# Pooled-key attention with a maxout layer: four of the first batch's twelve kv tiles are added by the loading DMAs

## The chip, the cores and the metric

The kernel runs on one core of a Trainium2 chip. The metric is the device time of one execution in microseconds (us); the median of 3 runs stands for a kernel. The engines are TensorE (PE in the profile; PEld is its weight load), VectorE (DVE), ScalarE (ACT), GpSimd (POOL) and SyncE (SP), which in this kernel only issues DMAs. The 16 DMA engines of the core are shared by everything that any engine issues.

## The reference

Keys and values are the same tensor: `kv` (4 batches, 384 x 32 positions, 128 channels), averaged over 4 x 4 windows and multiplied by `w_sr`. The queries attend to these 768 keys, and the result goes through a maxout layer with three weight matrices and an output matrix.

```
kv_pool = kv.reshape(B, H // 4, 4, W // 4, 4, C).mean(axis=(2, 4))
k = v = kv_pool.reshape(B, -1, C) @ w_sr
s = 1 / sqrt(C) * (q @ k.T);  a = exp(s - s.max(-1));  a /= a.sum(-1) + 1e-09
x = a @ v
out = max(x @ w1, x @ w2, x @ w3) @ w_out
```

There are 4 x 12288 queries, C is 128, and the hidden width is 768. All inputs and outputs are float32.

## The kernel before, in words

The queries are worked off in 96 groups of 512 (`G`). For each group there are score matmuls (token `S`), softmax on VectorE and ScalarE (`m`, `e`), splits into pairs of float16 (`c`, `l`), a DMA that transposes the weights of attention, the product with the values (`X`), the hidden layer (`H`, `R`, `M`, `C`, `L`) and the output product (`O`). Products are made of three float16 matmuls (high by high, high by low, low by high), which keeps nearly float32 accuracy.

The order of all work is written out by hand. Three tables of tokens, `START` (line 168), `STEADY` and `END`, are run by `run` (line 1165); each token calls one function. Every engine is wrapped in `InOrder` (line 98), so that it takes its instructions in the order in which the tokens issue them. All wrapped instructions carry line 106 of that helper, and are told apart in the profile by the names of their tiles. The chains between engines, the semaphores, follow from the tiles that an instruction reads and writes.

The change lies in `START`, in the preparation of the first batch's keys (class `Keys`, line 408). The batch's kv rows are cut in three parts s = 0, 1, 2 (`KS` = 3), and each part in four tiles i = 0 to 3, the four rows of a pooling window. A tile `pieces[s, i]` is 128 partitions of 1024 float32 (512 KB): two halves u of four neighbouring positions by 128 channels. What `START` does with them:

- `kv.s.i` (`load`, line 430): SP issues the load of a tile into a buffer of the pool `kvp` (13 buffers, line 82). Tile 2.2 is loaded in two halves. The same pool takes the eight 384 KB tiles of the layer's weights (`wd.n.h`, `load64`, line 248), which SP loads behind the kv tiles.
- `add.s.i.n` (`add`, line 442): tile n is added onto tile i, on VectorE, or on GpSimd with a `!`.
- `gat.s.i` (`gather`, line 464): TensorE multiplies each of a tile's eight 128 x 128 blocks with the identity and accumulates in PSUM. This sums what is left of the part and turns it, so that channels lie on partitions. One tile is 16 matmul instructions in the profile.
- `gd` and `gj`: ScalarE copies the sum out of PSUM (`pooled`), TensorE multiplies it by `w_sr`. `gp`, `gt`, `tops`, `sized` find a power of two for scaling, `gh` and `gl` split the keys into float16 pairs `k_hi`, `k_lo`. The first scores (`S`) need all parts.
- `fold`, `gb`: tile 2.0 is the late one (`LATE`, line 78); it is summed with 2.1 and 2.3 on VectorE, folded to half its width, and gathered last.
- `z` (`stir`, line 853): a matmul whose result nobody reads.

Before the change, parts 1 and 0 come first. SP loads 0.1, 1.3, 1.1, 1.0, 1.2, 0.3, 0.2, 0.0 and then the four tiles of part 2. In part 1 `add.1.2.3` adds tile 1.3 onto 1.2 (VectorE), `add.1.0.1!` adds 1.1 onto 1.0 (GpSimd), and 1.0 and 1.2 are gathered. In part 0 `add.0.2.3`, `add.0.0.1` and `add.0.0.2` sum all four tiles on VectorE into 0.0, which is gathered. GpSimd has before this the scaling of three half tiles of queries (`qc`), and after it the signs of the weights (`wn`). Later batches' keys are made in another way (`keys_step`, line 1141), spread over the steady part, and are not touched.

The weights are unpacked from pairs of 32-bit words by VectorE and ScalarE (`wm`, `ws`, `wl`, `wn`; tiles `w_e`), in `START`, between the softmax of the first groups.

Of the kernel before, what the change touches and what calls it, by code (L numbers as in the profile page):

```python
# [16 lines left out]
ALU = mybir.AluOpType  # L17
# [4 lines left out]
def kernel(  # L22
# [32 lines left out]
    B, N, C = q.shape  # L55
    _, HH, WW, _ = kv.shape
    R = 4
# [3 lines left out]
    P = 128  # L61
    NKT = NK // P
    NFT = DF // P
    G = 512
# [14 lines left out]
    KH, KW, KS, KU = 32, WB // 2, HB // 32, 2  # L79
# [6 lines left out]
    qp = ctx.enter_context(tc.tile_pool(name="qp", bufs=3))  # L86
# [11 lines left out]
    class InOrder:  # L98
# [9 lines left out]
    pe, dve, act, pool, sp_dma = (  # L108
        InOrder(e) for e in (nc.tensor, nc.vector, nc.scalar, nc.gpsimd, nc.sync)
    )  # L110
# [25 lines left out]
    def spread(out, t, n, start, stop):  # L136

        mm(out=out, lhsT=upper(t)[:, n:n + 1].to_broadcast([P, P]), rhs=upper(ident), start=start, stop=stop)
# [19 lines left out]
    wo = [const.tile([P, NFT // 2, 2, C], F16, name=f"wo{h}") for h in range(2)]  # L158
# [8 lines left out]
    TURNED = 2  # L167
    START = (
# [27 lines left out]
    )  # L196
    STEADY = (
# [28 lines left out]
    def sr_weights():  # L226
        e = prep.tile([C, C], F32, name="sr_e")
        dve.tensor_scalar(
            out=e.bitcast(I32), in0=wsr_sb.bitcast(I32), scalar1=0x7FFFFFFF, scalar2=None, op0=ALU.bitwise_and
        )  # L230
        ps = spare(True)
        mm(out=ps[:, :C], lhsT=ones, rhs=e, start=True, stop=True)
        pow2(col_row, ps[:, :C])
        dve.reciprocal(out=e, in_=col_row)
        dve.tensor_tensor(out=wsr_sb, in0=wsr_sb, in1=e, op=ALU.mult)
        ps = spare(True)
        mm(out=ps[:, :1], lhsT=col_row[:1], rhs=ones[:1, :1], start=True, stop=True)
        times(col, ps[:, :1], 1.0)
        times(col_ones, ones, col)
        W["sr"] = True  # L240
# [23 lines left out]
    tops = {}  # L264

    class Weights64:
# [13 lines left out]
        def load(self):  # L280
            self.r1, self.r0 = load64(self.w, self.h, self.wide)
# [126 lines left out]
    class Keys:  # L408
# [21 lines left out]
        def load(self, s, i, u=None):  # L430
            src = kv[self.b].rearrange("(s h i) (w r) c -> s i h w (r c)", s=KS, i=R, w=KW)[s, i]
            self.width.update({(s, i, n): R for n in (range(KU) if u is None else (u,))})
            if u is None:
                self.pieces[s, i] = kvp.tile([P, PIECE], F32, name="kv_piece")
                sp_dma.dma_start(out=self.pieces[s, i], in_=src)
                return
            if (s, i) not in self.pieces:
                self.pieces[s, i] = kvp.tile([P, PIECE], F32, name="kv_piece")
            part = slice(u * PIECE // KU, (u + 1) * PIECE // KU)
            sp_dma.dma_start(out=self.pieces[s, i][:, part], in_=src[:, :, part])  # L440

        def add(self, s, i, n, on=dve, us=slice(None)):
            view = lambda m: self.pieces[s, m].rearrange("p (u x) -> p u x", u=KU)[:, us]
            on.tensor_tensor(out=view(i), in0=view(i), in1=view(n), op=ALU.add)
            if self.first:
                assert all(self.width[s, i, u] == self.width[s, n, u] for u in range(KU)[us])
                assert not {(x, u) for x in (i, n) for u in range(KU)[us]} - self.left[s] - (self.late if s == LATE[0] else set())
                self.left[s] -= {(n, u) for u in range(KU)[us]}
# [404 lines left out]
    def stir(on=None):  # L853

        if on:
            return
        any_ = ones.bitcast(F16)
        mm(
            out=spare(False), lhsT=any_[:, :P], rhs=any_[:, :1].to_broadcast([P, G]), start=True, stop=True,
        )  # L860
# [235 lines left out]
    def start(token):  # L1096

        k, on = KT[0], dve if token[-1] == "!" else None  # L1100
        name, *n = token.rstrip("!").split(".")
        n = [int(x) for x in n]
        both = {"": slice(None), 0: slice(0, 1), 1: slice(1, 2)}
        if name == "sr":
            sr_weights()
        elif name == "kv":
            k.load(*n)
        elif name == "add":
            k.add(*n[:3], on=pool if on else dve, us=both[n[3] if n[3:] else ""])
        elif name == "fold":  # L1110
            k.fold(*n[:3], on=pool if on else dve, us=both[n[3] if n[3:] else ""])
        elif name == "gat":
            s, i, *u = n
            k.gather(s, i, u or range(KU))
        elif name in KEYS:
            getattr(k, KEYS[name])(*n, *([on] if on else []))
        elif name[0] == "w" and name[1:] in WEIGHTS:
            getattr(W[n[0], n[1]], WEIGHTS[name[1:]])(*([on] if on else []))
        elif name == "z":
            stir(on)  # L1120
        elif name in AIDS:
            AIDS[name](*n)
        else:
            step(name, on)
# [40 lines left out]
    def run(rows):  # L1165
        for row in rows:
            for token in row.split():
                start(token)
# [37 lines left out]
```

## Time and profile before

| | us |
|---|---|
| median of 3 runs | 1979.29 |
| lowest and highest run | 1977.48, 1981.5 |
| the profiled execution | 1975.92 |
| its span, first to last instruction | 1974.1 |

The profile is of that one execution. A row of the timeline or of the chain begins with its start in us from the span's start and its length in us; then engine, line, operation, written tile <- read tiles, shapes, and in brackets the idle time before it with what ended it. A row of the stretches gives for `A:B` the length, then the busy us (and the number of instructions) of PE, PEld, DVE, ACT and POOL, the granted TensorE clock, the mean busy share of the DMA engines and the GB/s that they moved. A row of a tile's instructions gives minimum, median and maximum length in ns, and first and last start; for DMA issues the line "DMA to landing" gives the us from the issue to the arrival of the last byte. A row of the groups gives busy us, mean ns of one, and the idle time before with what ended it. In the rows of DMA issues the last number is the median us to landing.

### The profile page before, as it was taken

The page shows a single profiled execution, that of the slowest core. Times are in us where ns is not written, and L with a number is a line of the kernel's source. Part 1 is how long each engine was busy: PE and PEld are TensorE (multiplying, and loading weights), DVE is VectorE, ACT ScalarE, POOL GpSimd, SP SyncE. Part 2 cuts the span into 40 slices and gives each one's busy share as a digit, 9 for nine tenths or more (in the row PEclk, how much of TensorE's full clock was granted, in tenths as well). Part 3 has the DMA queues.
Part 4 walks back from the last instruction along what each step waited for, and adds up shares of the span by engine and source line. Part 5 has one row for each costly group of instructions (what it writes and reads, how often), then busy time and mean ns, then how long its engine had stood idle before and what let it go on. Part 6 is the DMA issues. An engine that isn't in the chain of part 4 may idle for free.

```text
span 1974.1 us, 29441 instructions
## 1 busy us (share of the span) xinstructions
PE 1957.0 (99%) x9793; PEld 956.0 (48%) x9793; DVE 1447.5 (73%) x2523; ACT 1493.3 (76%) x2629; POOL 1311.5 (66%) x960
## 2 busy tenths in 40 slices
PE   7999999999999999999999999999999999999999
PEld 5444444444444444444444444444444444444444
DVE  8867777777767777777667777777766676766677
ACT  5777777777777777777777777777777777777775
POOL 4576766666667666766676677766676666666653
PEclk9999999999999999999999999999999999999999
DMA  9688777667677778766768767866776666766673
GB/s 280 126 157 165 154 148 142 142 132 143 128 149 166 155 145 160 144 129 136 137 132 166 155 147 157 169 122 128 137 143 137 131 127 127 146 122 125 131 129 81
DMA packets 842696, 283.97 MB, mean 144 GB/s; under 512 B 816048, under 2 KB 817200, under 8 KB 842544
## 3 DMA queue, kind: packets, MB, share of 16 engines
q1 hardware_dynamic: 842544, 282.09, 71.0%
q8 instruction: 77, 1.26, 0.3%
q14 instruction: 75, 0.61, 0.1%
HBM read 53.54 MB, written 25.17 MB: 40 GB/s over the span
## 4 chain that ended last, share of the span: by engine, by line
PE 98%; DMA 1%; DVE 0%; ACT 0%; SPq 0%; POOL 0%; issue 0%; ACTq 0%; POOLq 0%
PE ps_h L106 38%; PE ps_o L106 22%; PE ps_x L106 19%; PE ps_s L106 19%; DMA kv_piece<-in_kv_dram 0%; DMA aT<-ahl 0%; DMA kv_piece<-in_moe_w_dram 0%; SPq L106 0%; POOL kv_piece L106 0%; DVE w_e L106 0%; DVE ahl L106 0%; DVE mx L106 0%; ACT a L106 0%; ACT pooled L106 0%; ACT ahl L106 0%
## 5 line engine op out<-in xcount | busy, mean ns | idle before, releaser
L106 POOL TENSOR_TENSOR hl<-h,hh 128x512 f16<-128x512 f32 x474 | 565.9, 1199 | 508.0 <-ACT hh L106 496.8
L106 POOL TENSOR_TENSOR ahl<-a,ahl 128x768 f16<-128x768 f32 x378 | 627.7, 1681 | 99.5 <-ACT ahl L106 73.1
L106 DVE SCALAR_TENSOR_TENSOR h<-ps_h,h 128x512 f32<-128x512 f32 x575 | 396.4, 689 | 371.1 <-PE ps_h L106 213.2
L106 ACT ACTIVATE h<-ps_h 128x512 f32<-128x512 f32 x575 | 342.6, 596 | 282.9 <-PE ps_h L106 272.5
L106 PE MATMUL ps_h<-xh,d_hi 128*128 128x512 f16 x1150 | 435.8, 379 | 0.1
L106 PE MATMUL ps_h<-xl,d_hi 128*128 128x512 f16 x1150 | 435.8, 379 | 0.0
L106 PE MATMUL ps_h<-xh,d_lo 128*128 128x512 f16 x1150 | 435.8, 379 | 0.0
L106 DVE TENSOR_REDUCE mx<-ps_s 128x1 f32<-128x768 f32 x384 | 365.2, 951 | 51.8 <-PE ps_s L106 51.4
L106 ACT ACTIVATE a<-ps_s,nb,q_sc 128x768 f32<-128x768 f32 x384 | 379.2, 988 | 9.3 <-DVE nb L106 8.5
L106 PE MATMUL ps_s<-k_hi,qT 128*128 128x384 f16 x1536 | 374.8, 326 | 1.7 <-ACT a L106 1.7
L106 PE MATMUL ps_x<-aT,v_hi 128*128 128x512 f16 (+1 forms) x1188 | 366.7, 373 | 0.3 <-DMA aT<-ahl 0.2
L106 ACT CAST hh<-h 128x512 f16<-128x512 f32 x573 | 333.4, 613 | 40.0 <-DVE h L106 40.0
L106 PEld LDWEIGHTS <-d_hi 128*128 128x128 f16 x2308 | 225.8, 98 | 256.4
L106 PE MATMUL ps_o<-hh,wo 128*128 128x512 f16 x1140 | 339.1, 379 | 0.0
L106 PEld LDWEIGHTS <-qT 128*128 128x128 f16 x2304 | 225.2, 98 | 189.9 <-issue 2.3
L106 ACT CAST ahl<-a 128x768 f16<-128x768 f32 x379 | 309.6, 829 | 6.4 <-DMA aT<-ahl 0.6
L106 PEld LDWEIGHTS <-wo 128*128 128x128 f16 x1710 | 167.3, 98 | 192.1
L106 PE MATMUL ps_s<-k_lo,qT 128*128 128x384 f16 x768 | 250.4, 326 | 0.0
L106 PE MATMUL ps_x<-aT,v_lo 128*128 128x512 f16 (+1 forms) x594 | 220.2, 373 | 0.0
L106 PE MATMUL ps_o<-hl,wo 128*128 128x512 f16 x570 | 216.0, 379 | 0.0
L106 PEld LDWEIGHTS <-v_hi 128*128 128x128 f16 x1188 | 115.4, 98 | 134.3
L106 PEld LDWEIGHTS <-d_lo 128*128 128x128 f16 x1154 | 112.9, 98 | 121.8 <-issue 2.1
(154 smaller groups left out, 1422.8 us busy)
## 6 DMA issues: line engine op xcount, KB each, us to landing
q_sb<-in_q_dram SPq DMA_DIRECT2D x48, 512.0 KB, 4.3
out_dram<-o_sb SPq DMA_DIRECT2D x95, 256.0 KB, 2.0
kv_piece<-in_kv_dram SPq DMA_DIRECT2D x47, 512.0 KB, 4.5
aT<-ahl SPq DMA_TRANSPOSE x384, 4.0
kv_piece<-in_moe_w_dram SPq DMA_DIRECT2D x6, 384.0 KB, 7.9
o_turned<-o_planes SPq DMA_TRANSPOSE x95, 3.4
qT<-q_hl SPq DMA_TRANSPOSE x94, 3.6
kv_piece<-in_moe_w_out_dram SPq DMA_DIRECT2D x2, 384.0 KB, 6.7
```

Source lines behind the costliest of these rows:

```text
L106: return lambda **kw: tc.keep_in_program_order(op(**kw))
```

## The change

Tiles 1.0, 1.2, 0.2 and 0.0 are no longer loaded into buffers of their own. A new token `gain.s.i.n` loads tile n of part s onto tile i: a DMA begun by GpSimd with `accum_op` add, whose destination is the buffer in which tile i lies. It needs the landing of tile i first. Three VectorE additions and GpSimd's one go; of part 0 one VectorE addition is left, `add.0.1.3`. Gathered are 1.1, 1.3 and 0.1 in place of 1.0, 1.2 and 0.0. All other tokens and their order stay; the table is only broken into new lines. The first batch now uses 8 buffers of `kvp` in place of 12.

The new function, and its token:

```
+        def gain(self, s, i, n):
+
+            src = kv[self.b].rearrange("(s h i) (w r) c -> s i h w (r c)", s=KS, i=R, w=KW)[s, n]
+            pool.dma_start(out=self.pieces[s, i], in_=src, accum_op=ALU.add)
...
+            self.left[s] -= {(n, u) for u in range(KU)}
...
+        elif name == "gain":
+            k.gain(*n)
```

The table up to the gather of part 0:

```
-        "qp qv kv.1.1 kv.1.0 kv.1.2 add.1.2.3 qu qh add.1.0.1! gat.1.0 gat.1.2 qv kv.0.3 kv.0.2",
-        "add.0.2.3 gd.1 gj.1 z kv.0.0 add.0.0.1 add.0.0.2 gat.0.0 gp.1 kv.2.1 kv.2.0 add.2.0.1 kv.2.3 add.2.0.3",
+        "qp qv kv.1.1 gain.1.1.0 gain.1.3.2 qu qh gat.1.1 gat.1.3 qv kv.0.3 gain.0.3.2 gd.1 gj.1",
+        "z gain.0.1.0 add.0.1.3 gat.0.1 gp.1 kv.2.1 kv.2.0 add.2.0.1 kv.2.3 add.2.0.3 kv.2.2.0 gp.0 gat.2.2.0 kv.2.2.1",
```

More of the change, by code (lines that the diff above doesn't have):

```diff
@@ L440, in load @@
             sp_dma.dma_start(out=self.pieces[s, i][:, part], in_=src[:, :, part])
+        def gain(self, s, i, n):
+            src = kv[self.b].rearrange("(s h i) (w r) c -> s i h w (r c)", s=KS, i=R, w=KW)[s, n]
+            pool.dma_start(out=self.pieces[s, i], in_=src, accum_op=ALU.add)
+            assert {(x, u) for x in (i, n) for u in range(KU)} <= self.left[s] and (s, n) not in self.pieces
+            self.left[s] -= {(n, u) for u in range(KU)}
         def add(self, s, i, n, on=dve, us=slice(None)):
```

47 rows, old and new, of the table START are left out of this document.

## The prediction

> **What bounds the kernel now.** I read the page first (shares of the engines, the 40 slices, the queues), then the stretches of the first 60 us, then the chain that ended last, and last the timelines and landings of the transfers that the change touches.
>
> ```profile
> span 1974.1 us, 29441 instructions
> PE 1957.0 (99%) x9793; PEld 956.0 (48%) x9793; DVE 1447.5 (73%) x2523; ACT 1493.3 (76%) x2629; POOL 1311.5 (66%) x960
> PE   7999999999999999999999999999999999999999
> PE 98%; DMA 1%; DVE 0%; ACT 0%; SPq 0%; POOL 0%; issue 0%; ACTq 0%; POOLq 0%
> q1 hardware_dynamic: 842544, 282.09, 71.0%
> ```
>
> TensorE is the bound from the second slice on: the chain runs 98% through it. The span holds 1974.1 - 1957.0 = 17.1 us in which TensorE does nothing, and the only slice below 9 tenths is the first. So the change can move only the opening, and what it moves there goes through to the end, since behind the opening there is no slack on TensorE to take it up. All transfers so far go through one queue, q1; none is begun by GpSimd.
>
> ```profile
> core 0: us, PE busy (x) PEld busy (x) DVE busy (x) ACT busy (x) POOL busy (x), PEclk, DMA share, GB/s
> 8.00:12.00 4.00, 2.09 (x10) 2.12 (x11) 2.76 (x8) 0.84 (x3) 0.88 (x1) 1.00 1.01 406
> 14.00:16.00 2.00, 1.00 (x9) 1.00 (x10) 2.00 (x2) 0.83 (x2) 0.95 (x1) 1.00 1.01 414
> 20.00:22.00 2.00, 2.00 (x18) 1.79 (x16) 1.97 (x4) 0.00 (x0) 0.00 (x0) 1.00 1.04 391
> 26.00:28.00 2.00, 1.57 (x9) 0.82 (x7) 1.90 (x8) 2.00 (x6) 0.58 (x1) 1.00 1.03 399
> 30.00:40.00 10.00, 7.95 (x40) 3.54 (x39) 9.48 (x19) 8.45 (x15) 5.62 (x5) 1.00 0.91 191
> ```
>
> Two things are full at once in the opening: the 16 DMA engines (share 1.01 to 1.04, 391 to 414 GB/s, from 8 to 28 us), and VectorE. The chain through it:
>
> ```profile
> 4.18 8.29 DMA kv_piece<-in_kv_dram
> ...
> 12.60 2.36 POOL kv_piece L106
> 14.96 0.04 issue
> 15.00 3.85 PE ps_s L106 x32
> 18.88 0.38 ACT pooled L106
> 19.26 0.04 issue
> 19.30 0.70 PE ps_s L106 x2
> 20.00 0.22 PE ps_x L106
> 20.22 2.05 PE ps_s L106 x16
> 22.26 2.02 PE ps_x L106 x16
> ```
>
> The fourth kv tile (1.0) lands at 12.5, GpSimd's addition of 1.0 onto 1.1 ends at 14.96, TensorE gathers tiles 1.0 and 1.2 from 15.00, projects, and gathers 0.0 from 20.22 and 2.2 from 22.26. TensorE takes this in the written order. Its second condition is VectorE:
>
> ```profile
> 13.84 2.19 DVE L106 TENSOR_TENSOR kv_piece<-kv_piece 128x1024 f32<-128x1024 f32 x1 [0.53 <-DMA kv_piece<-in_kv_dram]
> 16.55 3.60 DVE L106 TENSOR_TENSOR kv_piece<-kv_piece 128x1024 f32<-128x1024 f32 x3
> 20.41 2.48 DVE L106 TENSOR_TENSOR kv_piece<-kv_piece 128x1024 f32<-128x1024 f32 x2
> 23.14 0.68 DVE L106 TENSOR_TENSOR kv_piece<-kv_piece 128x512 f32<-128x512 f32 x1
> ```
>
> The three additions of s = 0 end at 16.55 + 3.60 = 20.15, which releases the gather at 20.22; those of s = 2 and the fold follow without a pause to 23.82. One undisturbed addition is 3.60 / 3 = 1.20 us.
>
> **What the change removes.** Three VectorE additions (of 1.3, and two of the three of s = 0: 2.19 + 2 x 1.20 = 4.6 us) and GpSimd's (2.36 us). One VectorE addition stays, 0.1 with 0.3, and it now needs two accumulated tiles. SP issues four 512 KB loads fewer, so s = 2 and the weights move up four places in its queue.
>
> **What it adds.** Four loads of the same bytes that GpSimd begins, each after the landing of the tile onto which it adds. When can the first begin? The third tile of SP's queue, 1.1, keeps its place.
>
> ```profile
> L106 SPq DMA_DIRECT2D kv_piece<-in_kv_dram x1: 680/680/680, 3.5 to 3.5; - x1
> ...
> DMA to landing us min/median/max: 7.7/7.7/7.7
> ...
> L106 SPq DMA_DIRECT2D kv_piece<-in_kv_dram x1: 535/535/535, 13.8 to 13.8; - x1
> ...
> DMA to landing us min/median/max: 9.0/9.0/9.0
> wsr_sb<-in_w_sr_dram SPq DMA_DIRECT2D x1, 64.0 KB, 1.8
> kv_piece<-in_kv_dram SPq DMA_DIRECT2D x47, 512.0 KB, 4.5
> kv_piece<-in_moe_w_dram SPq DMA_DIRECT2D x6, 384.0 KB, 7.9
> 27.42 3.01 POOL L106 TENSOR_TENSOR w_e<-w_e,w_s 128x384 f32<-128x384 f32 x3 [12.47 <-PE ps_o L106]
> ```
>
> Tile 1.1 lands at 3.5 + 7.7 = 11.2; the last one (second half of 2.2) at 13.8 + 9.0 = 22.8. Between them lie nine tiles' worth: (22.8 - 11.2) / 9 = 1.29 us for 512 KB while the engines are full, which is the 406 GB/s of the stretches. GpSimd is free: after its old addition it stands idle for 12.47 us until 27.42, so issuing four transfers there holds up nobody, unless they were still waiting then. Issue and landing around the bytes: the 64 KB load took 1.8 us, of which 0.16 is its bytes at that rate, leaving 1.6 us. I charge this once, since later accumulations queue behind the first.
>
> **The time of the four accumulations.** This the trace doesn't show, and it is bounded from both sides. The lower end: no sharing, no price for the addition, 11.2 + 1.6 + 1.29 = 14.1 for the first and 11.2 + 1.6 + 4 x 1.29 = 18.0 for the fourth. Then the gather of 1.1 starts 0.9 us before 15.00, and the last addition ends at 18.0 + 1.2 = 19.2, 0.95 before 20.15: a gain of 0.9 us, which is the most that this change can bring. But at 11.2 SP still has kv tiles 0.3, 2.1, 2.0, 2.3, 2.2 and five weight tiles in line, 5 + 5 x 0.75 = 8.75 tiles of 512 KB. They use the same 16 full engines. If both streams move turn about, each accumulated tile costs its own time plus one tile of SP's. With an accumulation at the price of a plain load: 2 x 1.29 = 2.58 per tile, the fourth lands at 11.2 + 1.6 + 10.3 = 23.1. An accumulation also has to read the 512 KB that lie in SBUF; if these cost as much as the 512 KB from HBM, a tile takes 3 x 1.29 = 3.87, and the fourth lands at 28.3. I take the middle, a weight of 1.5: 2.5 x 1.29 = 3.2 per tile, landings at 16.0, 19.2, 22.5 and 25.7. The nearest row is the plain load, but nothing makes the second read free, and nothing says that it takes the HBM's part of the path.
>
> The Trainium skill (DMA: Bandwidth & Descriptors, Queues, rings and completion order) says that each DMA engine goes round robin between the rings that have work, a packet at a time; with one queue in the trace no row here can show it, and by it the sum is the one with turns. The same page (Anatomy of one DMA) gives a transfer begun by GpSimd 2.0 us and its bytes at 436 GB/s, so by it an undisturbed accumulation would land 3.2 us after 11.2, at 14.4.
>
> **What waits.** TensorE: gather of 1.1 at 16.0 instead of 15.00, of 1.3 at 19.2, projection to about 22.7, then it stands until the addition of 0.1 and 0.3 ends. VectorE has this addition queued ahead of the peak of s = 1, both additions and the fold of s = 2, the late tile's peak and the weights' first steps; all of them wait with it. It ends at 25.7 + 1.2 = 26.9. Old place 20.15, so both chains are 26.9 - 20.15 = 6.7 us late; SP's stream moves one tile per accumulated one, so four by 25.7 and the fifth, 2.2, 1.29 later at 27.0, in time for its gather behind that of 0.1; the weights behind it need no buffer to come free (8 kv tiles and 5 of weights fill the pool of 13) and are no later than the chains that use them. ScalarE's copies come behind the gathers and keep their distance.
>
> From there the opening is a chain through TensorE, VectorE (9.48 of 10 us busy from 30 to 40) and ScalarE without slack, so the delay arrives whole at the scores:
>
> ```profile
> 28.10 0.50 PE L106 MATMUL ps_s<-k_hi,qT 128*128 128x384 f16 x2
> ```
>
> They go from 28.10 to 34.8. The 4.6 us that VectorE saves lie ahead of the addition that waits, and buy nothing.
>
> **The sum.** Removed work 0 (off the end's path), the four accumulations +6.7, GpSimd's and SP's freed time 0. The profiled execution took 1975.9 us, span 1974.1 and 1.8 around it; it would take 1975.9 + 6.7 = 1982.6. The median of the runs is 1979.3, 3.4 above, and I set the forecast on it: **1986.0 us**. A difference of 0.2%, 4.0 us, is about what a measurement of this kernel can tell from none; the three runs of before are themselves 4 us apart.
>
> **The rivals.**
>
> *The accumulations are hidden (same).* If the queue of GpSimd gets well over half of the engines, or SP's stream yields because its outstanding loads are limited, the fourth tile lands before 23.0, the delay stays under 23.0 + 1.2 - 20.15 = 4.0, and at 18.9 it is nothing: 1978.4 to 1983.3. The point that decides is a cost per accumulated tile of (23.0 - 12.8) / 4 = 2.55 us. For it: a plain price with equal turns lies at 2.58, just on that point. Against it: the full engines, and the second read. Chance 0.24.
>
> *TensorE goes slow in its waits.* The trace has the same 128x128 f32 matmuls at two speeds:
>
> ```profile
> L106 PE MATMUL ps_h<-sr_e,q_sb 128*128 128x128 f32 x16 | 3.7, 424 | 5.0 <-DVE sr_e L106 5.0
> L106 PE MATMUL ps_s<-ident,kv_piece 128*128 128x128 f32 x32 | 3.8, 278 | 1.4 <-POOL kv_piece L106 1.4
> ```
>
> Sixteen take 3.7 us after 5.0 us of standing still, but half of 3.8 after 1.4. With the forecast's landings TensorE stands about 2.5 us before 16.0 and 4 us before the gather of 0.1; two gathers at the slow pace cost 2 x (3.7 - 1.9) = 3.6 more, 10.3 in all: 1989.6. The Trainium skill (TensorE: Matmul & The Clock Gate, What's actually happening) states that after an idle window of some 3.4 us the array runs at half its clock. By that rule this happens before the gather of 0.1; the two rows agree with it, while the granted clock reads 1.00 in every stretch above. Against: work between shortens the waits. Chance 0.12.
>
> *The accumulation is much dearer,* three reads' worth per tile with turns: 4 x 1.29 = 5.2 each, the fourth at 33.4, 14.5 late: 1993.8. For it: no row bounds it. Chance 0.10.
>
> **How the numbers follow.** Forecast (2.58 to 3.87 us per tile, 4.1 to 9.4 late, 1983.4 to 1988.7) 0.50; hidden 0.24; slow array 0.12; dear accumulation 0.10; 0.04 for something faster by over 0.2% that these views don't show, since the bound of the gain is 0.9. So slower 0.50 + 0.12 + 0.10 = 0.72, same 0.24, faster 0.04. The range takes the hidden case from its lower part, 1979.0, up to the dear one, 1994.0; about 0.15 lies outside.
>
> **What would show it.** Right: a second queue with four 512 KB transfers of 8 us and more from issue to landing, VectorE's one remaining addition of s = 0 waiting on a DMA and ending near 27, an idle stretch of TensorE before the third gather, first scores near 35, everything behind them shifted by the same amount. Wrong: an accumulation that costs 2.55 us or less per tile (first scores before 32), or a delay at the scores that the stretch from 30 to 60 us takes back.

## The result and the profile after

| | before | after |
|---|---|---|
| median of the runs (4 each), us | 1979.16 | 1990.51 |
| lowest and highest run | 1977.48, 1981.5 | 1989.36, 1991.96 |
| the profiled execution | 1975.92 | 1989.36 |
| its span | 1974.1 | 1987.2 |

The ratio of the times is 1.0057 (95% interval 1.0039 to 1.0074): slower by 11.35 us, where 6.7 were forecast. The profile page after, in its header, its first strip, the new queue and the chain's shares:

```profile
span 1987.2 us, 29433 instructions
PE   5999999999999999999999999999999999999999
q0 software_dynamic: 576, 2.10, 0.5%
PE 97%; DMA 2%; DVE 1%; ACT 0%; SPq 0%; POOL 0%; issue 0%; DVEq 0%; ACTq 0%
```

Of TensorE's strip only the first slice has changed, 5 tenths for 7, and the chain has one per cent more of DMA and of VectorE, for one less of TensorE. The new queue q0 carries 2.10 MB, the four tiles. The chain of waits up to the third and fourth gathers:

```profile
3.46 7.53 DMA kv_piece<-in_kv_dram
...
11.30 1.81 POOL kv_piece L106 x2
13.11 17.84 DMA kv_piece<-in_kv_dram
...
31.04 1.24 DVE kv_piece L106
...
32.32 3.19 PE ps_s L106 x16
35.51 2.29 PE ps_x L106 x16
```

It no longer runs through GpSimd's addition and the gathers of part 1, but through the fourth accumulating DMA alone: 17.84 us from the issue to the landing at 30.95. GpSimd's issues of these four, and their landings:

```profile
L106 POOL DMA_DIRECT2D kv_piece<-in_kv_dram x4: 1026/1411/1974, 11.3 to 13.1; - x4
...
DMA to landing us min/median/max: 9.1/13.4/17.8
```

All four are issued between 11.3 and 13.1; they land at 20.4, 23.9, 27.5 and 30.9, 3.5 us apart. What waits for that, from the timelines of VectorE and TensorE:

```profile
31.04 1.23 DVE L106 TENSOR_TENSOR kv_piece<-kv_piece 128x1024 f32<-128x1024 f32 x1 [15.97 <-DMA kv_piece<-in_kv_dram]
```
```profile
20.46 6.58 PE L106 MATMUL ps_s<-ident,kv_piece 128*128 128x128 f32 x32 [6.75 <-DMA kv_piece<-in_kv_dram]
32.32 3.19 PE L106 MATMUL ps_s<-ident,kv_piece 128*128 128x128 f32 x16 [3.90 <-DVE kv_piece L106]
35.30 2.49 PE L106 MATMUL ps_x<-ident,kv_piece 128*128 128x128 f32 x16
41.53 0.50 PE L106 MATMUL ps_s<-k_hi,qT 128*128 128x384 f16 x2
```

VectorE stands 15.97 us for its one addition, which ends at 32.27 (before: the last of part 0 at 20.15). The third gather starts at 32.32, before at 20.22: 12.1 later. It and the fourth take 3.19 and 2.29 us in the chain, before 2.05 and 2.02: 1.4 more. The first scores start at 41.53, before at 28.10: 13.4 later, and the span is 13.1 longer. So all of it arises in the first 42 us; behind that, 0.3 us are given back between these two profiles.

The stretches of after show the engines behind it:

```profile
12.00:14.00 2.00, 1.72 (x9) 1.42 (x7) 1.01 (x3) 0.83 (x2) 2.00 (x4) 1.00 1.02 418
18.00:20.00 2.00, 0.00 (x0) 0.00 (x0) 0.00 (x0) 0.00 (x0) 0.00 (x0) 1.00 1.05 253
28.00:30.00 2.00, 0.42 (x2) 0.00 (x0) 0.00 (x0) 0.00 (x0) 0.00 (x0) 1.00 1.02 264
34.00:36.00 2.00, 2.00 (x12) 2.00 (x11) 1.45 (x3) 0.00 (x0) 0.00 (x0) 0.50 0.13 47
```

From 18 to 20 no engine computes. The DMA engines are busy all the time (share 1.05), yet move 253 GB/s where the same share carried 391 to 414 before. From 34 to 36 they are nearly idle (0.13): the loads are through, and what the first scores still need is computation alone.

### The profile page after: what moved, and what is told of

It reads as the page before. It is cut to its first block, busy times and chain, and to the rows that moved or that the text cites. A ratio compares the mean times of both kernels' runs of the same rounds, so it can differ in the third digit from the quotient of the medians.

```text
span 1987.2 us, 29433 instructions
## 1 busy us (share of the span) xinstructions
PE 1961.3 (99%) x9793; PEld 960.2 (48%) x9793; DVE 1447.6 (73%) x2520; ACT 1493.6 (75%) x2629; POOL 1314.0 (66%) x963
## 3 DMA queue, kind: packets, MB, share of 16 engines
q8 instruction: 77, 1.26, 0.3%
## 4 chain that ended last, share of the span: by engine, by line
PE 97%; DMA 2%; DVE 1%; ACT 0%; SPq 0%; POOL 0%; issue 0%; DVEq 0%; ACTq 0%
PE ps_h L106 37%; PE ps_o L106 22%; PE ps_x L106 19%; PE ps_s L106 19%; DMA kv_piece<-in_kv_dram 1%; DMA aT<-ahl 0%; DMA kv_piece<-in_moe_w_dram 0%; DVE mx L106 0%; SPq L106 0%; POOL kv_piece L106 0%; DVE w_e L106 0%; DVE kv_piece L106 0%; ACT a L106 0%; DVE d_lo L106 0%; DVE ahl L106 0%
## 6 DMA issues: line engine op xcount, KB each, us to landing
kv_piece<-in_kv_dram POOLq DMA_DIRECT2D x4, 512.0 KB, 13.4
```

## The experiments

The theory: the gather of part 0 is late by the landing of the fourth accumulation; that landing is made of a lead of GpSimd's transfer (the time from issue to landing that the bytes do not explain), of the accumulation's second read, which fills the DMA engines as its bytes do, and of turns with SP's queue. Rivals: GpSimd's queue is slow by itself; the accumulation is dear and the sharing is not, or the reverse; TensorE's slow pace makes up the time.

The table of tokens is shown below in extracts: lines are joined, their ends are left away, and rows of `z` are written as a product. Each ratio is taken against runs of before made beside that kernel (medians 1978.9 to 1980.7 us).

**Without the addition.** Copies in place of accumulations, so four tiles' sums are left out; the waits and the queues stay.

```
-            pool.dma_start(out=self.pieces[s, i], in_=src, accum_op=ALU.add)
+            pool.dma_start(out=self.pieces[s, i], in_=src)
```

> The changed kernel, but GpSimd's four transfers copy instead of adding, so the sums of four tile pairs are left out; waits, queues and order stay. Double-price theory (an accumulation fills the DMA engines for its bytes twice, once for HBM and once for the tile in SBUF, turn about with SP's stream): the fourth tile lands 4 x 1.29 = 5.2 us earlier, near 25.8 in place of 30.9; from 16 to 24 us the engines move about 400 GB/s again in place of 260; first scores near 36.4; time about 5 us below the changed kernel. Rival (the price lies in GpSimd's queue itself, the addition is free): the fourth lands near 30.9 again, 260 GB/s, first scores near 41.5, time as the changed kernel's.

1984.95 us, ratio 1.0032 (1.0019 to 1.0044); first scores at 34.10, earlier than the 36.4 expected. The tile's row and two stretches of this kernel:

```profile
DMA to landing us min/median/max: 7.1/9.5/12.0
```
```profile
18.00:20.00 2.00, 1.60 (x7) 1.60 (x8) 0.00 (x0) 0.00 (x0) 0.00 (x0) 1.00 1.04 410
22.00:24.00 2.00, 2.00 (x11) 2.00 (x11) 0.00 (x0) 0.00 (x0) 0.00 (x0) 1.00 1.02 401
```

The fourth lands at 25.15 in place of 30.95, 2.27 us apart in place of 3.5, and the engines are back at 400 GB/s and more. The addition's own price is 5.8 us at the landing and 7.4 at the scores (34.10 for 41.53), since the third and fourth gathers were also quicker, together by 1.6 us. In the medians it is 5.6, with intervals that leave some 4 us either way. The other half, 6.0 us against before, comes with no addition at all.

**Without the sharing.** SP's loads behind tile 0.3 wait until the fourth accumulation has landed: a 512-byte DMA of SP's reads the finished tile first. The one addition now sums into 0.3, and that is gathered.

```
-z gain.0.1.0 add.0.1.3 gat.0.1 gp.1 kv.2.1
+z gain.0.1.0 hold add.0.3.1 gat.0.3 gp.1 kv.2.1
...
+        elif name == "hold":
+            sp_dma.dma_start(out=prep.tile([P, P], F32, name="hold")[:1], in_=k.pieces[0, 1][:1, :P])
```

> The changed kernel, but SP's loads behind tile 0.3 wait until the fourth accumulation has landed, so that the four run without SP's stream. Double-price theory: 2 x 1.29 = 2.6 us per tile, DMA share near 1 at about 200 GB/s, the fourth lands near 14.5 + 10.3 + 1.6 = 26.4. Rival (sharing is all, the addition is free): 1.3 us per tile, about 400 GB/s, the fourth lands near 21.3. Rival (GpSimd's queue has a pace of its own): 3.5 us per tile as before, the fourth near 30.9, DMA share well under 1. The other tiles come after, so the whole is no faster than the changed kernel by more than 3 us in any of them, and up to 5 us slower.

1993.18 us, ratio 1.0074 (1.0059 to 1.0089). The tile's row, a stretch, VectorE's row and a row of TensorE in this kernel:

```profile
DMA to landing us min/median/max: 5.6/8.3/11.2
```
```profile
18.00:20.00 2.00, 2.00 (x12) 2.00 (x11) 0.00 (x0) 0.00 (x0) 0.00 (x0) 0.54 1.07 211
```
```profile
24.12 1.23 DVE L106 TENSOR_TENSOR kv_piece<-kv_piece 128x1024 f32<-128x1024 f32 x1 [9.42 <-DMA kv_piece<-in_kv_dram]
```
```profile
33.38 3.71 PE L106 MATMUL ps_x<-ident,kv_piece 128*128 128x128 f32 x16 [5.31 <-DMA kv_piece<-in_kv_dram]
```

Alone on the engines the four land at 16.6 to 24.0, one per 2.5 us, at a share of 1.07 and 211 GB/s. The addition starts 6.9 us earlier than in after, as the turns fall away. The time is nevertheless no better: part 2, held back, is late now (its gather waits 5.31 us for a load, to 33.38), and the first scores start at 40.83.

**Neither addition nor sharing.** The same with copies; again four sums are left out.

> As the run with SP's stream held until the fourth transfer has landed, but the four copy instead of adding (four sums are left out). Double-price theory: 1.29 us per tile, full share at about 400 GB/s, the fourth lands at 11.0 + 2.7 + 5.2 = 18.9, 5.1 before the held accumulations' 24.0; first scores 35.7. Rival (GpSimd's queue is slow by itself, whatever it does): the fourth not before 22, DMA share well under 1 between 13 and 19 us.

1988.45 us, ratio 1.0039 (1.0025 to 1.0053); the fourth lands at 19.4, near the 18.9 expected, and the first scores start at 37.83, 2.1 later than the 35.7 expected. The tile's row and a stretch of this kernel:

```profile
L106 POOL DMA_DIRECT2D kv_piece<-in_kv_dram x4: 543/556/727, 11.1 to 12.9; - x4
...
DMA to landing us min/median/max: 4.5/5.4/6.5
```
```profile
16.00:18.00 2.00, 2.00 (x11) 2.00 (x11) 0.00 (x0) 0.00 (x0) 0.00 (x0) 1.00 1.01 416
```

GpSimd's queue alone moves a tile in 1.26 us, 416 GB/s: it is not slow. From issue to the first landing it takes 4.5 us, so 4.5 - 1.26 = 3.2 us go before and around the bytes. Together the first three kernels and after give, for 512 KB begun by GpSimd:

| us from tile to tile | alone | beside SP's queue |
|---|---|---|
| copied | 1.26 | 2.27 |
| added | 2.5 | 3.5 |

Down a column the addition costs 1.2, one more tile's time; across a row SP's turns cost 1.0. The two add up. The traces show both prices directly: packets, MB and share of the DMA engines by queue (q0 GpSimd's, q1 SP's), first of after from the landing of the second accumulated tile to that of the third (23.89 to 27.45), then of the copies beside SP's queue (20.61 to 22.88):

```profile
q0 software_dynamic: 145, 0.53, 74.3%
q1 hardware_dynamic: 146, 0.40, 31.1%
```
```profile
q0 software_dynamic: 144, 0.52, 57.7%
q1 hardware_dynamic: 144, 0.39, 44.7%
```

The queues move packet for packet. An accumulated tile fills the engines for 0.743 x 3.56 = 2.65 us, a copied one for 0.577 x 2.27 = 1.31. SP's packets are those of the weights, 0.40 MB in place of 0.52: this is why a turn costs 1.0 us and not a whole tile's time.

**The queue without addition and without waiting.** The kernel before; GpSimd begins the loads of 1.0, 1.2, 0.2 and 0.0 at 9.1 to 10.8 into buffers of their own, and all of before's additions stay.

```
-qp qv kv.1.1 kv.1.0 kv.1.2 add.1.2.3
+qp qv kv.1.1 pkv.1.0 pkv.1.2 pkv.0.2 pkv.0.0 add.1.2.3
...
-kv.0.3 kv.0.2 add.0.2.3 gd.1 gj.1 z kv.0.0 add.0.0.1
+kv.0.3 add.0.2.3 gd.1 gj.1 z add.0.0.1
...
-                sp_dma.dma_start(out=self.pieces[s, i], in_=src)
+                by.dma_start(out=self.pieces[s, i], in_=src)
```

> The kernel before, with its four loads of 1.0, 1.2, 0.2 and 0.0 begun by GpSimd into buffers of their own, without addition and without a wait for another tile; all additions stay. Double-price theory: same bytes, same full engines, so the last of all tiles lands near 23 as before; order between the two streams shifts, first scores between 28 and 31, time within 3 us of the kernel before. Rival (GpSimd's queue itself is slow or starts 5 us late): tile 0.0 lands beyond 26, first scores beyond 34, time 6 us and more above.

1985.07 us, ratio 1.0031 (1.002 to 1.0043): not within 3 us of before, and the scores not by 31: the expectation missed. The rival has the time right (6 us and more), not the landings (0.0 beyond 26). GpSimd's row, VectorE's row and the first scores of this kernel:

```profile
16.61 2.33 POOL L106 TENSOR_TENSOR kv_piece<-kv_piece 128x1024 f32<-128x1024 f32 x1 [5.21 <-DMA kv_piece<-in_kv_dram]
```
```profile
22.93 2.48 DVE L106 TENSOR_TENSOR kv_piece<-kv_piece 128x1024 f32<-128x1024 f32 x2 [0.85 <-DMA kv_piece<-in_kv_dram]
```
```profile
33.23 0.50 PE L106 MATMUL ps_s<-k_hi,qT 128*128 128x384 f16 x2
```

The bytes are the same and the engines as full (about 405 GB/s), yet tile 1.0 lands at 16.6 in place of 12.5, and 0.0 at 22.9 in place of 17.5. In one queue the tiles land in the order written; with two, every second turn goes to SP's, where part 2 and the weights stand, which nobody needs yet. Of the 5.4 us by which 0.0 is late, 4.1 are there at the first tile already: GpSimd issues it at 9.1, and the first packet of its queue moves only at 13.1, when before had tile 1.0 landed. The other 1.3 are the turns. So a second queue costs some 6 us here with no accumulation in it. The copies above cost as much, though they begin 2 us later and spare additions; that both have the same parts is not shown.

**One part at a time.** After with part 1 as before, and after with part 0 as before:

```
-kv.1.1 gain.1.1.0 gain.1.3.2 qu qh gat.1.1 gat.1.3
+kv.1.1 kv.1.0 kv.1.2 add.1.2.3 qu qh add.1.0.1! gat.1.0 gat.1.2
```

> Part 1 as in the kernel before, only part 0 with its two accumulations. Double-price theory (turn about with SP, 3.87 us per accumulated tile, some 4.1 us from the first begin to the first byte's share): the first must wait for tile 0.3, now sixth in SP's queue, at 15.0; the second lands at 15.0 + 4.1 + 7.7 = 26.8, the third gather starts at 28.1 in place of 20.2, first scores at 36.0 plus up to 1.4 for a slow TensorE, time 8 us above the kernel before. Rival (half of the change costs half): first scores at 34.8, time 5.7 above.

```
-gat.1.3 qv kv.0.3 gain.0.3.2 gd.1 gj.1 z gain.0.1.0 add.0.1.3 gat.0.1
+gat.1.3 qv kv.0.3 kv.0.2 add.0.2.3 gd.1 gj.1 z kv.0.0 add.0.0.1 add.0.0.2 gat.0.0
```

> Part 0 as in the kernel before, only part 1 with its two accumulations. Double-price theory: the second lands at 11.3 + 4.1 + 7.7 = 23.1, its gather ends near 25, the third gather starts near 26.4 in place of 20.2, first scores at 34.3, time 6 us above the kernel before. Together with the other half this is more than the whole, since the halves' waits overlap in the whole. Rival (the harm is only in the last tile, that of part 0): first scores below 31.

Part 0 alone: 1988.32 us, ratio 1.0038 (1.0023 to 1.0053), some 7.5 us; the two land 12 us after issue at the latest, the addition starts at 27.87, the scores at 38.34, later than the 36.0 to 37.4 expected (the third gather took 3.64 us). Part 1 alone: 1987.43, ratio 1.0033 (1.0022 to 1.0044), 6.5 us where 6 were expected; scores 36.05, where 34.3 were. In the time the two sum to 14 us for the whole's 11.35, which the intervals don't tell apart. At the scores they do: 10.2 and 8.0 late, 18.2 together, for the whole's 13.4. The late start is paid in each, since the first accumulated tile lands 9.2 and 9.5 us after its issue, as in after (9.1), and in the whole only once.

**One accumulation, begun early and with time in hand.** The kernel before, with 2.1 accumulated onto 2.0 at 9.2, and tile 0.1 moved ahead of 0.0 in SP's queue:

```
-qc qc qc kv.0.1 qp! qt
+qc qc qc kv.2.0 gain.2.0.1 qp! qt
...
-gj.1 z kv.0.0 add.0.0.1
+gj.1 z kv.0.1 kv.0.0 add.0.0.1
...
-gp.1 kv.2.1 kv.2.0 add.2.0.1 kv.2.3
+gp.1 kv.2.3
```

> The kernel before with one accumulation, of a tile that is needed late and begun early: tile 2.0 is loaded first in place of 0.1, GpSimd adds 2.1 onto it by DMA from 8.9 us, one VectorE addition goes. Double-price theory: it lands near 8.9 + 4.1 + 3.9 = 16.9, long before its use near 22, and still costs, because the engines are full to 28 us and it fills them 1.29 us longer: SP's tiles behind it land 1.3 later, and first scores come at 29.4, up to 30.5 where the turns delay parts 1 and 0; time 1 to 2.5 us above the kernel before. Rival (an accumulation with time in hand is free): first scores at 28.1, within 0.4.

1983.79 us, ratio 1.0018 (1.0009 to 1.0027), some 3.6 us; scores at 33.74, where 29.4 to 30.5 were expected. VectorE's row of this kernel:

```profile
21.99 2.49 DVE L106 TENSOR_TENSOR kv_piece<-kv_piece 128x1024 f32<-128x1024 f32 x2 [1.35 <-DMA kv_piece<-in_kv_dram]
```

The accumulated tile itself lands at 19.2 (16.9 was expected), before it is needed. But SP's 0.0 lands at 21.9 in place of 17.5: 4.4 later. One more tile stands ahead of it (1.3), and the other 3.1 are near the 2.5 for which an accumulation alone fills the engines. A plain load of 2.1 begun as early would also have filled them for 1.3, so that the addition's share is some 1.2 to 1.8; this kernel changes the order of the loads as well, and does not part the two. What it shows is that a transfer which nobody waits for yet is not free while the engines are full; that the addition makes it dearer rests on the table above. At the scores, 5.6 us late, the slow gathers add to it (5.19 us for the first two, 3.48 for the third).

**TensorE kept awake.** After with 20 stirring matmuls ahead of the first gather and 15 ahead of the third, then with 8 ahead of the third alone:

```
-"qu qh gat.1.1"
+"qu qh " + "z " * 20 + "gat.1.1"
...
-"add.0.1.3 gat.0.1"
+"add.0.1.3 " + "z " * 15 + "gat.0.1"
```

> The changed kernel with 20 matmuls that nobody reads ahead of the first gather and 15 ahead of the third, to keep TensorE from standing still. If the slow pace of TensorE after its waits adds to the delay: 32 gathers back from 6.6 to 3.8 us, 16 of the third from 3.2 to 2.05, first scores at 41.5 - 1.1 - 0.3 = 40.1, time 1.4 us below the changed kernel (the first two gathers' 2.7 us lie in the wait for the fourth tile and buy nothing). If the slow pace costs nothing, or isn't cured by this: scores at 41.5 as before.

```
-"add.0.1.3 gat.0.1"
+"add.0.1.3 " + "z " * 8 + "gat.0.1"
```

> The changed kernel with 8 matmuls that nobody reads ahead of the third gather only, which end near 32 when it may start. If the slow pace of TensorE after its wait is part of the delay: the third gather back from 3.2 to 2.0 us and the fourth from 2.3 to 2.0, so first scores 1.1 to 1.4 us nearer to the addition that they follow: 9.1 to 9.4 us from that addition's start instead of 10.5 (the kernel before: about 9.2 from the start of its last addition of part 0). If not: 10.5 again. In the time this is at the edge of what can be told.

The first: 1990.86 us, ratio 1.0062 (1.0047 to 1.0077). The gathers were back at 3.98 us for two and 1.95 for one, but the stirring ran past the addition's end, and the third gather began 1.4 us after it: inconclusive. The second: 1990.39, ratio 1.0056 (1.0042 to 1.007). VectorE's row, and TensorE's rows of this kernel:

```profile
30.73 1.23 DVE L106 TENSOR_TENSOR kv_piece<-kv_piece 128x1024 f32<-128x1024 f32 x1 [15.82 <-DMA kv_piece<-in_kv_dram]
```
```profile
32.01 2.05 PE L106 MATMUL ps_s<-ident,kv_piece 128*128 128x128 f32 x16 [0.68 <-DVE kv_piece L106]
33.89 1.95 PE L106 MATMUL ps_x<-ident,kv_piece 128*128 128x128 f32 x16
39.59 0.50 PE L106 MATMUL ps_s<-k_hi,qT 128*128 128x384 f16 x2
```

From the start of the addition to the scores it takes 8.86 us, in after 41.53 - 31.04 = 10.49. The slow pace is worth 1.6 us at the scores, a little more than the 1.1 to 1.4 expected. In the median of the runs this can't be seen.

**The swap without DMAs.** To see whether the additions' places matter at all: the kernel before, with both additions of part 1 on VectorE, that of 1.1 onto 1.0 first; GpSimd adds nothing.

```
-kv.1.2 add.1.2.3 qu qh add.1.0.1! gat.1.0
+kv.1.2 add.1.0.1 qu qh add.1.2.3 gat.1.0
```

> The kernel before with the first two additions exchanged: VectorE adds 1.1 onto 1.0, GpSimd adds nothing, VectorE then adds 1.3 onto 1.2. If work is to be taken off the first link of the chain without new DMA work, this does it: the first gather starts at 12.5 + 0.8 + 1.2 = 14.6 in place of 15.0. But the third gather hangs on the landing of tile 0.0 at 17.5 and two additions, 19.9 to 20.2, so first scores move by 0.2 at most: no measurable difference. Rival (VectorE is the bound of the opening, one more addition on it costs 1.2): first scores at 29.3.

1977.97 us, ratio 0.9991 (0.9982 to 1.0): no difference that can be told. TensorE's row of this kernel:

```profile
14.56 5.96 PE L106 MATMUL ps_s<-ident,kv_piece 128*128 128x128 f32 x32 [0.83 <-DVE kv_piece L106]
```

The gather starts 0.4 us earlier than in before and then runs slowly, 5.96 us for 3.85; the scores start at 29.42, not at the 28.1 to 28.3 expected. That is the rival's 29.3, but not for its reason: VectorE ended the additions of part 0 at 19.9 and then stood 1.83 us for TensorE.

**Both kernels again.** Is the gathers' pace, and with it a part of the 13.1 us between the two profiles, chance from execution to execution? Before and after, unchanged, profiled once more.

> The kernel before once more, unchanged, for a second profile. The first profile's execution took 1975.9 us, 3 us under the median of its runs, and its first 32 gathers ran at the fast pace (3.84 us), which the run with the exchanged additions did not (5.96 us) after a like wait. If TensorE's pace at that point is a matter of chance between executions: 32 gathers between 5 and 6.5 us here, first scores between 29 and 30.5, span 1976 to 1979. If it belongs to the kernel: 3.84 us and 28.1 again.

> The changed kernel once more, unchanged. The four accumulations land as before, the first near 20.4 and the fourth near 30.9, each within 0.5; first scores between 40 and 41.6, depending on the pace of the third gather (2.05 or 3.2 to 3.6 us); span 1986 to 1990.

Before: 1979.56 us, span 1977.8; the first gathers took 3.84 us again and the scores started at 28.28. That they are slow by chance in the same program is not borne out. The 3.7 us between the two executions of before come later, at a DMA that transposes attention weights and at the matmuls behind it, in the chain of waits of the first execution and of this one:

```profile
42.33 3.75 DMA aT<-ahl
...
46.12 1.17 PE ps_x L106 x18
```
```profile
42.45 5.63 DMA aT<-ahl
...
48.12 2.08 PE ps_x L106 x18
```

The transpose takes 1.9 us longer, and TensorE, which has stood 2.12 us for it, works at near half pace behind it (granted clock 0.50 from 48 to 50): 0.9 us in these 18 matmuls and 0.6 in the next.

After again: 1991.78, span 1989.7, the landings (9.1 to 17.9 us after issue), the addition (31.30) and the scores (41.80, a little over the 40 to 41.6 expected) as in its first profile, and the same transpose at 5.82 us where its first profile has 3.7; its matmuls then ran at full pace. So each kernel has executions with this transpose about 2 us longer; of the fourteen profiles of this document ten have it at 5.5 to 5.8. Between the two profiles with the short one the spans differ by 13.1 us, between the two with the long one by 1989.7 - 1977.8 = 11.9, near the 11.35 of the medians.

From the first scores to the first product of the hidden layer (`ps_h<-xh,d_hi`) it takes 21.6 us in before, 25.0 in its second execution, 21.5 and 23.6 in the two of after. Behind that product every profile here, of whatever kernel, has 1924.1 to 1924.6 us left. So nothing takes the delay of the scores back or adds to it but this one stretch, and there it is the execution that differs, by up to 3.9 us over all kernels. A time compared by a few runs carries that; the start of the first scores does not.

## Why the prediction was right, and where its sizes were off

- **What bounds the kernel.** Right: the first scores are 13.4 us late, the span 13.1, and the second slice on is full in both. Behind the opening nothing took the delay back.
- **The forecast's own bounds.** Its branch was 4.1 to 9.4 us late, 1983.4 to 1988.7 us. The gather is 12.1 late and the median 1990.51, beyond them, and inside the whole range only because that reached up to the dear accumulation. The path and the wait were right; the landing was 5.2 us out.
- **When the accumulations begin.** Right: 11.3 for 11.2.
- **"Issue and landing around the bytes ... 1.6 us".** Too small. It was taken from a load that SP begins; one that GpSimd begins takes 3.2 (the kernel with neither addition nor sharing): +1.6.
- **"I take the middle, a weight of 1.5".** Too small: the second read weighs as much as the first, 2.5 us for 1.26 alone on the engines. With turns the sum by weight 2 was 3.87 per tile; 3.5 were measured, since SP's turns, of the weights' smaller packets, cost 1.0 and not 1.29. Against 3.2 that is 4 x 0.3 = +1.2.
- **The first tile.** Missing from the sum: the first of the four lands 9.1 us after its issue, of which 3.2 are the lead and 3.5 its own interval. The other 2.4 are new. With copies beside SP's queue they are 7.1 - 3.2 - 2.27 = 1.6, with accumulations alone on the engines 5.6 - 3.2 - 2.5 = -0.1; so they come with the sharing. The traces put them ahead of the first byte: the first packet of GpSimd's queue moves at 15.75 in after, 4.5 us after the first issue, and at 12.70 where SP is held, 1.7 us after it. Until 15.7 SP's queue has the engines full (share 1.015 from 11 to 15.7). That the first turn has to wait for what SP's queue has already handed to the engines fits this, but is an argument, not shown.

The three make 1.6 + 1.2 + 2.4 = 5.2: the fourth landing at 30.9 for 25.7.

- **Turns between the queues.** Right in kind: one transfer of SP's for each accumulated tile. In the trace of after, the second half of 2.2 and two tiles of weights land at 22.3, 25.8 and 29.3, between the accumulated tiles at 20.4, 23.9, 27.5 and 30.9. A turn is lighter than thought, 1.0 us, but with the late start the sharing costs 6.9 us at the addition (31.04 for 24.12). The rule of the Trainium skill (DMA: Bandwidth & Descriptors, Queues, rings and completion order), round robin between the rings with work, agrees: 145 packets to 146 between two landings.
- **What waits.** Right in kind: VectorE stood 15.97 us and then added, and its saved additions bought nothing; in the swap kernel one addition more on VectorE and none on GpSimd left the time as it was. GpSimd's issues held up nobody: it stood idle for 25.86 us behind them.
- **The slow array.** It was put as a rival of 3.6 us in two gathers; it happened on top of the forecast, at 1.6 us (the 8 stirs) in the third and fourth gather. Its time, 1989.6, is the nearest of all to the result, but by luck: it is made of a delay of 6.7 and a slow pace of 3.6, where 12.1 and 1.4 to 1.6 were measured. The first two, 6.58 us for 3.85, were hidden in the wait for part 0.
- **The sum.** Late at the gather by 12.1 (5.2 over the 6.7 forecast, and 0.2 in the gaps), at the scores by 13.4, in the medians by 11.35. Before's median of 1979.16 lies by its execution with the long transpose (1979.56), after's 1990.51 between its two (1989.36 and 1991.78), so the medians are nearer together than the first two profiles. How often each kernel has the long transpose and the slow pace behind it, four runs don't tell; at the scores the delay is 13.4 and 13.5 in the two pairs of profiles.
- **The rivals.** *Hidden* falls: its point was 2.55 us per tile, and it was 3.5. Copies without addition, at 2.27 per tile, would have passed that point and still cost 6 us, for the lead and the first turn, which the point left out. *Much dearer* (5.2 per tile) falls too, though its time of 1993.8 is closer to the result than its price.

Not settled: why the first gathers run slowly after waits of 0.8 to 1.7 us in some kernels (swap 5.96 us, one accumulation 5.19) and at 3.84 in before, twice, after 1.4 to 1.7; what the first packet of GpSimd's queue waits for; and why the transposes differ. The Trainium skill (TensorE: Matmul & The Clock Gate, What's actually happening) states that the window by which the clock is set runs on freely, so that where in it the work begins matters; that would let short waits end either way, but no run here shows the window.

## What to carry to other kernels

A DMA that adds while it loads is no free addition where the DMA engines are full: it costs them two tiles' time for one (2.65 us for 1.31), and here the engine that it relieved had 16 us to spare. A second queue also costs by itself: it ends the written order of landing, so what is urgent shares turn about with what is not, and its first packet moved 3.9 to 4.5 us after the issue in the kernels with a busy SP queue, 1.4 to 1.7 alone. Before moving work between engines, follow the one tile that the critical path waits for, and count what is ahead of it and beside it in the queues.

## What the runs showed of the hardware

- An accumulating DMA counts its bytes once and fills the engines as for twice: 211 GB/s at a share of 1.07, against 416 at 1.01 for copies.
- GpSimd's issues of accumulations are longer in the profile, 1.03 to 1.97 us each against 0.53 to 0.73 for a copy, but overlap: four begin within 1.8 us either way, and all four last 3.78 us against 2.33. From issue to landing the first 512 KB transfer alone on the engines took 4.5 us (copied) and 5.6 (added). The Trainium skill (DMA: Bandwidth & Descriptors, Anatomy of one DMA) gives 2.0 us and the bytes at 436 GB/s, from which one would estimate 3.2 in all; these runs do not bear that out.
- The granted clock of a stretch does not show every slow gather: in after it reads 1.00 over the first two gathers (6.58 us), in its second execution 0.50 over the same two (6.69 us), and in both 0.50 at 34 to 36, where the third ends and the fourth begins. Of after's first profile:

```profile
20.00:22.00 2.00, 1.53 (x7) 1.54 (x8) 0.00 (x0) 0.00 (x0) 0.00 (x0) 1.00 1.06 255
22.00:24.00 2.00, 2.00 (x11) 2.00 (x11) 0.00 (x0) 0.00 (x0) 0.00 (x0) 1.00 1.05 262
```

Where a gather's pace matters, its length over the number of its matmuls tells it: 6.58 / 32 = 0.21 us here, 3.85 / 32 = 0.12 in before.
